# Reordering the first row of attention before a long matrix product: values between scores, a last block on ScalarE, and the dilated half of x first

## The chip, the cores and the metric

The kernel runs on one core of a Trainium2 chip. The metric is the device time of one execution in microseconds (us). Executions of one kernel agree within about half a microsecond to two microseconds here, so every comparison below is between runs taken in the same rounds on the same chip. The parts of the core that matter are TensorE (PE in the profile; PEld is its weight load), VectorE (DVE), ScalarE (ACT), GpSimd (POOL), SyncE (SP), and the DMA engines.

## The reference

Attention over eight batch elements ("rows" 0 to 7 below), eight heads of 64 columns, 576 tokens, followed by a feed-forward layer with a squared ReLU.

```python
mask_plain = (rel >= 0) & (rel < 32)                        # heads 0-3: "sliding"
mask_dil   = (rel >= 0) & (rel < 128) & (rel % 4 == 0)      # heads 4-7: "dilated"
attn = softmax(where(mask, q @ k.T / 8, -1e9))              # per row and head
x = (attn @ v).transpose(0, 2, 1, 3).reshape(4608, 512)     # 8 rows x 576 tokens
h = x @ w_in                                                # 512 -> 2048
return (relu(h) ** 2) @ w_out                               # 2048 -> 512
```

## The kernel before

The feed-forward layer takes tokens in chunks of 512. Its first product, mm1, makes `ph` from `xT`, which is x transposed, in four blocks of 128 columns. Blocks 0 and 1 are the sliding half (transposed into PSUM, an on-chip memory, as `px`, then copied by ScalarE), and blocks 2 and 3 are the dilated half (`py`, copied the same way). `po`, and `poa` to `poe`, are results of the second product; VectorE combines them (`u`), and `otl` and `otu` are parts of the output that are then stored. While one chunk's products run, the attention of the next row is woven in: `pump(n)` advances the products by n steps, a step being two matmuls of mm1 or four of the second product. In rows 2 to 7, `attn_values` calls a small function between its pieces (a fill), and that function pumps.

```python
def mm1_gen(c, g, sm=None):                 # chunk c
    xs = xT[:, :, c * TOKC : (c + 1) * TOKC]
    for ffc in range(NFF):                  # 16 blocks of w_in
        ph = pmool.tile(...)
        for dmk in range(NDM):              # 0, 1 sliding; 2, 3 dilated
            nc.tensor.matmul(ph, wi[:, dmk, ...], xs[:, dmk, :],
                             start=(dmk == 0), stop=(dmk == NDM - 1))
            if dmk == 1:
                yield
        relu_squared(c, ffc, g, ph, rts)
        # ... cut
        yield

def normalize(b, what, pav, w, n=2):        # divide by the softmax's sum, on VectorE
    # ... cut: x, rcp, pv
    nc.vector.reciprocal(rcp[0:w, 0:n], pv[:, :, :, D])
    nc.vector.tensor_tensor(out=x[0:w, 0:n], in0=pv[:, :, :, 0:D], in1=rcp..., op=ALU.mult)
```

Row 0 has nothing to run beside. It is a prologue, with idle matmuls (`pj`) that have no use but to keep TensorE busy. Its second half reads as follows; `s_` are scores, `av_` value products with their normalization, and `x_` the transposes and copies.

```python
    s_sliding_half(0, 1)
    s_sliding_half(1, 1)
    cast_dilated_v(nc.gpsimd, DIL, (1,)); cast_sliding_v(nc.gpsimd, 3, 3, 6)
    constants_late()
    idle(8)
    zs = av_dilated(0, 1, 0)
    x_dilated(0, 0, ys, False)
    zs += av_dilated(0, 1, 1)
    xs += av_sliding(0, 3, 5)
    xs += av_sliding(0, 5, 6)
    idle(16); x_dilated(0, 1, zs, False)
    idle(16); x_sliding(0, 1, xs, False)
    idle(12)
    # ... then mm1 of chunk 0, with row 1's attention woven in
```

The softmax here doesn't subtract the row's maximum and nothing guards it: scores larger than these inputs give would overflow.

## Time and profile before

| | before |
|---|---|
| median of the first three runs | 307.59 us (306.98 to 307.77) |
| profiled execution: first to last instruction | 306.2 us, mean granted clock 0.997 |
| TensorE busy | 97% |
| first `ph` of row 0's chunk | 25.29 us |
| from it to the first `ph` after row 1 | 37.43 us |
| from the end of VectorE's last instruction to the end | 4.3 us |

The table reads in the order of the program. TensorE has no free time worth speaking of, so the time of the kernel is a sum: the prologue to 25.29 us, then matmuls, then what TensorE waits for between them, then an ending after the last matmul.

### The profile page before, as it was taken

Reading aid. Unit: us, or ns where it says so; the run is one execution under the profiler, and the core shown is the slowest. Engines: PE = TensorE matmul, PEld = TensorE weight load, DVE = VectorE, ACT = ScalarE, POOL = GpSimd, SP = SyncE. Lnnn points to the kernel's source line nnn. Section 1 sums busy time; section 2 is a strip of 40 time slices with the busy share of each in tenths; the row PEclk is TensorE's granted clock in tenths of the full one; section 3 lists DMA queues with packets and bytes.
Section 4 is the critical chain, followed back from the end, with each engine's and each line's share of the span. In section 5 each row is a group of like instructions: output and inputs, shape, how many; then the busy total and the mean of one; then the engine's idle time right before and its main releaser. Section 6 shows DMA issues by size and latency. Waiting matters only on the chain.

```text
span 306.2 us, 7007 instructions
## 1 busy us (share of the span) xinstructions
PE 295.5 (97%) x2898; PEld 192.3 (63%) x2898; DVE 208.6 (68%) x410; ACT 184.4 (60%) x304; POOL 49.7 (16%) x98
## 2 busy tenths in 40 slices
PE   7989999999998999999999999999999999999993
PEld 3766444444795469646964696469646974784583
DVE  4662375679975797679767976797669775743843
ACT  6565776678925992499248934893489346306610
POOL 7465000208005000410041003200100010000000
PEclk9999999999999999999999999999999999999998
DMA  8999997899989999889938983999410021003013
GB/s 172 223 213 228 235 206 155 154 174 220 317 180 273 222 177 222 256 161 206 225 128 173 228 204 119 181 195 199 144 44 0 2 88 51 2 0 137 2 34 104
DMA packets 85615, 47.89 MB, mean 156 GB/s; under 512 B 68112, under 2 KB 82896, under 8 KB 85200
## 3 DMA queue, kind: packets, MB, share of 16 engines
q1 hardware_dynamic: 76688, 27.24, 41.2%
q0 software_dynamic: 8352, 19.80, 29.2%
q10 hardware_dynamic: 544, 0.43, 0.5%
q8 instruction: 22, 0.36, 0.5%
q14 instruction: 9, 0.07, 0.1%
HBM read 39.85 MB, written 16.52 MB: 184 GB/s over the span
## 4 chain that ended last, share of the span: by engine, by line
PE 90%; DMA 2%; DVE 2%; ACT 2%; issue 1%; POOL 1%; ACTq 0%; POOLq 0%
PE ph L380 41%; PE poa L430 9%; PE pob L430 9%; PE pod L430 5%; PE poe L430 4%; PE poc L430 4%; PE po L401 3%; DMA early<-in_q_dram 2%; PE paw L764 2%; PE pav L747 2%; PE pz L667 2%; PE ps L648 1%; PE pj L530 1%; PE px L779 1%; PE py L797 1%
## 5 line engine op out<-in xcount | busy, mean ns | idle before, releaser
L380 PE MATMUL ph<-xT,wi 128*128 128x512 f16 x576 | 130.0, 379 | 0.3 <-ACT xT L803 0.3
L346 ACT ACTIVATE rt<-ph 128x512 f16<-128x512 f32 x144 | 84.9, 601 | 36.2 <-PE ph L380 35.9
L380 PEld LDWEIGHTS <-wi 128*128 128x128 f16 x576 | 54.4, 98 | 63.0 <-issue 0.8
L350 DVE TENSOR_TENSOR g<-rt 128x1024 f16<-128x1024 f16 x63 | 43.6, 692 | 46.4 <-ACT rt L346 46.2
L430 PEld LDWEIGHTS <-sm 128*128 128x128 f16 x512 | 46.9, 98 | 4.8
L430 PEld LDWEIGHTS <-g 128*128 128x128 f16 x384 | 36.0, 98 | 6.9 <-DVE g L348 1.3
L430 PE MATMUL pob<-T,sm 128*128 128x256 f16 x256 | 32.8, 272 | 0.0
L430 PE MATMUL poa<-wo,g 128*128 128x256 f16 x256 | 32.6, 273 | 0.0
L450 POOL DMA_DIRECT2D out_dram<-otl x6 | 4.6, 761 | 149.2 <-DVE otl L485 132.3
L803 ACT COPY xT<-py 128x576 f16<-128x576 f16 x16 | 10.2, 639 | 27.9 <-PE py L797 27.7
L728 DVE TENSOR_TENSOR x_d<-paw,rcp_d 72x512 f16<-72x512 f32 x32 | 22.0, 686 | 1.1
L785 ACT COPY xT<-px 128x576 f16<-128x576 f16 x16 | 10.3, 641 | 14.6 <-PE px L779 14.5
L620 ACT ACTIVATE AT<-pz 128x576 f16<-128x576 f32 x28 | 16.7, 649 | 1.9 <-PE pz L667 1.5
L401 PE MATMUL po<-wo,g 128*128 128x512 f16 x64 | 17.8, 379 | 0.0
L728 DVE TENSOR_TENSOR x_p<-pav,rcp_p 96x512 f16<-96x512 f32 (+1 forms) x25 | 16.6, 665 | 0.9
L620 ACT ACTIVATE AT<-ps 128x576 f16<-128x576 f32 x28 | 16.7, 649 | 0.8 <-PE ps L630 0.4
L430 PE MATMUL poe<-wo,sm 128*128 128x256 f16 x128 | 16.5, 273 | 0.0
L430 PE MATMUL poc<-T,sm 128*128 128x256 f16 x128 | 16.4, 272 | 0.0
L727 DVE RECIPROCAL rcp_d<-paw 72x8 f32<-72x8 f32 x32 | 6.3, 197 | 14.6 <-PE paw L764 14.6
L430 PE MATMUL pod<-T,g 128*128 128x256 f16 x128 | 16.1, 272 | 0.0
L621 DVE TENSOR_TENSOR AT<-AT,maskp 128x576 f16<-128x576 f16 x28 | 12.7, 457 | 2.8 <-ACT AT L620 1.8
L470 ACT COPY otu<-poa 128x512 f32<-128x512 f32 x8 | 4.7, 586 | 16.1 <-PE poa L430 16.1
(119 smaller groups left out, 352.0 us busy)
## 6 DMA issues: line engine op xcount, KB each, us to landing
sv<-in_v_dram SPq DMA_DIRECT2D x40, 128.0 KB, 4.7
sd<-in_v_dram SPq DMA_DIRECT2D x8, 512.0 KB, 6.8
dk<-in_k_dram POOLq DMA_DIRECT2D x12, 288.0 KB, 6.1
dk<-in_q_dram POOLq DMA_DIRECT2D x12, 288.0 KB, 7.5
out_dram<-otl POOLq DMA_DIRECT2D x6, 512.0 KB, 3.3
out_dram<-otu POOLq DMA_DIRECT2D x6, 512.0 KB, 4.3
sd<-in_v_dram SPq DMA_DIRECT2D x8, 288.0 KB
wi<-in_moe_w_in_dram POOLq DMA_DIRECT2D x4, 512.0 KB, 9.9
```

What stands on the lines that cost most here:

```text
L346: nc.scalar.activation(rt[:, o, :], ph[:], ACTF.Relu)
L350: nc.vector.tensor_mul(g[:, ffc - 1 : ffc + 1, :], rt, rt)
L380: nc.tensor.matmul(ph, wi[:, dmk, ffc * P : ffc * P + P], xs[:, dmk, :], start=(dmk == 0), stop=(dmk == NDM - 1),)
L401: nc.tensor.matmul(po, g[:, ffc, t * P : (t + 1) * P], wo[:, ffc, :], start=(ffc == 0), stop=(ffc == NFF - 1),)
L430: nc.tensor.matmul(acc, lhs[:, k, t * P : (t + 1) * P], rhs[:, k, :], start=(first and k == 0), stop=(k == NK - 1), skip_group_check=True,)
L620: nc.scalar.activation(AT[:, u, 0:UW], ps[:, :, 0 : UW // 2], ACTF.Exp, scale=scale)
L621: nc.vector.tensor_mul(AT[:, u, 0:UW], AT[:, u, 0:UW], mask)
L667: nc.tensor.matmul(ps[:, e, QD * n : QD * (n + 1)], QKTd[r, 1, a, q0 - PADD : q0 - PADD + P], QKTd[r, 0, a, q0 : q0 + QD], start=True, sto ...
L727: nc.vector.reciprocal(rcp[0:w, 0:n], pv[:, :, :, D])
L728: nc.vector.tensor_tensor(out=x[0:w, 0:n], in0=pv[:, :, :, 0:D], in1=rcp[0:w, 0:n].unsqueeze(3).to_broadcast([w, n, HH, D]), op=ALU.mult,)
L785: nc.scalar.copy(xT[:, 0:2, t0 : t0 + 288], px[:, 0:UW].rearrange("x (c t) -> x c t", c=2),)
L803: nc.scalar.copy(xT[:, 2:4, t0 : t0 + 288].rearrange("x c (i r) -> x c i r", r=DIL), py[:, 0:UW].rearrange("x (c r i) -> x c i r", c=2, r= ...
```

## The change

The intent is to shorten the prologue. The first value product of the second half goes between the two late score tiles. The last block of 96 tokens is normalized by four ScalarE instructions instead of one on VectorE. The last cast of q is split by head pairs over GpSimd and VectorE. And mm1 takes the dilated blocks first, because in row 0 the dilated half is ready before the sliding half. A slower pumping at the end of row 2 is added to go with the new order of mm1.

```diff
@@ the last cast, split
-    cast_sliding_qk_half(0, 1, nc.gpsimd)
+    cast_sliding_qk_pair(0, 1, 1, nc.gpsimd)
 ...
     ys = av_dilated(0, 0, 0)
+    cast_sliding_qk_pair(0, 1, 0, nc.vector)
@@ mm1
-            for dmk in range(NDM):
+            for n, dmk in enumerate((2, 3, 0, 1)):
 ...
-                    start=(dmk == 0), stop=(dmk == NDM - 1),
+                    start=(n == 0), stop=(n == NDM - 1),
@@ normalize
-    def normalize(b, what, pav, w, n=2):
+    def normalize(b, what, pav, w, n=2, eng=None):
 ...
+        if eng is nc.scalar:
+            for h in range(HH):
+                nc.scalar.mul(x[0:w, 0, h, :], pv[:, 0, h, 0:D], rcp[0:w, 0, h : h + 1])
+            return [x[:, 0]]
@@ row 0, second half
     s_sliding_half(0, 1)
-    s_sliding_half(1, 1)
     cast_dilated_v(nc.gpsimd, DIL, (1,))
     cast_sliding_v(nc.gpsimd, 3, 3, 6)
-    constants_late()
-    idle(8)
+    idle(4)
     zs = av_dilated(0, 1, 0)
+    s_sliding_half(1, 1)
     x_dilated(0, 0, ys, False)
+    idle(4)
     zs += av_dilated(0, 1, 1)
     xs += av_sliding(0, 3, 5)
-    xs += av_sliding(0, 5, 6)
+    xs += av_sliding(0, 5, 6, nc.scalar)
+    constants_late()
     idle(16)
@@ rows 2 to 7
-        attn_values(b, lambda: pump(2))
+        n_val[0] = 0
+        def rows():
+            n_val[0] += 1
+            pump(1 if b == 2 and n_val[0] > 7 else 2)
+        attn_values(b, rows)
```

(Cut: the definition of the split cast, and the passing of `eng` through `av_sliding`.)

More of the change, by code (lines that the diff above doesn't have):

```diff
@@ L184, in cast_sliding_qk_half, with cast_sliding_qk_pair @@
             sq[:, i, :, 192 * f : 192 * (f + 1)].rearrange("p h (j d) -> p j h d", d=D),
+        )
+    def cast_sliding_qk_pair(i, f, hp, eng):
+        hs = slice(2 * hp, 2 * hp + 2)
+        copy(
+            eng,
+            nqh[:, f, i, :, hs, :],
+            sq[:, i, hs, 192 * f : 192 * (f + 1)].rearrange("p h (j d) -> p j h d", d=D),
         )
@@ L383, in mm1_gen @@
                     xs[:, dmk, :],
-                    start=(dmk == 0),
-                    stop=(dmk == NDM - 1),
+                    start=(n == 0),
+                    stop=(n == NDM - 1),
                 )
-                if dmk == 1:
+                if n == 1:
                     yield
@@ L734, in normalize, with av_sliding @@
         return [x[:, i] for i in range(n)]
-    def av_sliding(b, m0, m1):
+    def av_sliding(b, m0, m1, eng=None):
         if m1 - m0 == 2:
@@ L753, in av_sliding @@
                 )
-        return normalize(b, f"p{m0}", pav, QB, m1 - m0)
+        return normalize(b, f"p{m0}", pav, QB, m1 - m0, eng)
     def av_dilated(b, t, a):
```

## The prediction

> **What bounds the kernel now.** I began with the page's first part, busy time by engine.
>
> ```profile
> PE 295.5 (97%) x2898; PEld 192.3 (63%) x2898; DVE 208.6 (68%) x410; ACT 184.4 (60%) x304; POOL 49.7 (16%) x98
> ```
>
> TensorE is the bound. A change can pay only where TensorE waits, or runs matmuls that exist to keep it busy. I then asked for the busy time of stretches cut where a token chunk's first product (ph) begins, and kept these four. The first two numbers are the stretch's length and TensorE's busy time.
>
> ```profile
> 0.00:25.29 25.29, 21.30 (x334) 15.24 (x335) 13.69 (x44) 15.14 (x27) 15.12 (x30) 1.00 1.11 202
> ...
> 62.72:95.25 32.53, 31.68 (x320) 21.13 (x318) 27.14 (x52) 21.37 (x35) 7.69 (x11) 1.00 1.01 230
> 95.25:125.85 30.60, 30.60 (x315) 20.69 (x315) 22.84 (x44) 20.23 (x33) 3.47 (x9) 1.00 1.06 223
> 125.85:156.73 30.88, 30.88 (x318) 20.81 (x316) 23.54 (x45) 20.23 (x33) 4.62 (x10) 1.00 0.85 191
> ```
>
> From 95 us on TensorE has no hole until the last store. The end is therefore the start of ph at 25.29, plus fixed work, plus the holes before 95 us. Row 0 (the first batch element's attention) is the prologue, a chain of latencies padded with idle matmuls. The chain that ended last shows its tail:
>
> ```profile
> 18.38 0.57 issue
> 19.80 0.55 PE pj L530 x8
> 20.88 0.69 DVE x_d L728
> 21.72 0.54 PE pav L747 x12
> 22.26 0.89 PE pj L530 x16
> 23.41 0.90 PE pj L530 x16
> 24.60 0.65 ACT xT L785
> 25.29 13.97 PE ph L380 x64
> ```
>
> Two waits and 44 idle matmuls set 25.29. The value product pav waits for its PSUM buffer, which VectorE's scaling x_d frees. After it come 16 idle matmuls, a transpose, 16 idle, the last transpose (px) and its copy xT, for which ph waits while 12 idle matmuls run.
>
> Last, the timeline at the ends of rows 1 and 2, for the reordered product:
>
> ```profile
> 61.72 1.40 ACT L803 COPY xT<-py 128x576 f16<-128x576 f16 x2
> ...
> 62.01 0.43 PE L797 MATMUL py<-ident,x_d 72*128 72x72 f16 x8
> ...
> 62.72 0.59 PE L380 MATMUL ph<-xT,wi 128*128 128x512 f16 x2
> ...
> 93.47 0.69 DVE L728 TENSOR_TENSOR x_d<-paw,rcp_d 72x512 f16<-72x512 f32 x1
> ...
> 94.22 0.30 PE L797 MATMUL py<-ident,x_d 72*128 72x72 f16 x4 [0.55 <-DVE x_d L728]
> 94.36 0.60 PE L380 MATMUL ph<-xT,wi 128*128 128x512 f16 x2
> 94.56 0.64 ACT L803 COPY xT<-py 128x576 f16<-128x576 f16 x1 [0.79 <-PE py L797]
> 95.25 4.91 PE L380 MATMUL ph<-xT,wi 128*128 128x512 f16 x22 [0.29 <-ACT xT L803]
> ```
>
> In every row after row 0 the dilated half of x (copied from py) lands last, and ph takes the sliding half first. Two ph matmuls, 0.43 us at 0.216 each, hide the copy: wholly at 62.72 (the copy ends at 63.12, the third ph is due at 63.15), and in part at 94.36. In row 0 alone the sliding half lands last.
>
> **What the Trainium skill says.** (1) "TensorE: Matmul & The Clock Gate", Back-to-back issue gap: warm spacing N/2.4 + 2.5 ns, so 216 ns at 512 columns and 56 at 128. The trace agrees: 64 ph matmuls in 13.81 us (216 ns), 16 idle ones in 0.89 us (56). (2) "ScalarE: Activation LUTs", What ACT_TABLE_LOAD costs: 186 ns + 0.833 N, some 93 ns more per pointer operand, and 93 ns of overlap between neighbours. The trace has a 576-column copy at 0.64 us (formula 0.67), a 288-column one at 0.40 (0.43), and two of these in 0.70, an overlap of 0.10. No run so far shows the pointer term. (3) "Runtime: NRT & Kernel Launch", Instruction fetch mechanics: instructions arrive by DMA in blocks of 256. The "issue" gap of 0.57 us, in the middle of six alike score matmuls, after some 441 TensorE instructions and with the DMA full, looks like a late block; the trace does not prove it.
>
> **The change, part by part.**
>
> *Casts.* GpSimd casts half of the last q block, some 0.45 us for 0.82, and issues the second pair of w_in loads some 0.37 us sooner. VectorE takes the other half, some 0.5 us, at 15.5 between two scalings. Its next product is due at 16.27, so both casts land in time. Gain on the path: 0.
>
> *Values between the scores.* The first late score tile (ps) still runs at 18.95 and its exponential at 19.25 to 19.87. Now the first value product (paw) follows after 4 idle matmuls, at 19.34 instead of 20.19. VectorE scales it from 20.0 to 20.7, and the second paw finds its buffer free at 20.97. But the second score tile, moved behind the first paw, needs the PSUM buffer that the exponential frees: it starts at 19.92, its scores at 20.27, its exponential at 20.62 to 21.26. So pav starts at 21.30, not 21.72. Gain: 0.42.
>
> *Last block on ScalarE.* VectorE ends the second x_d at 22.35, the next scaling at 23.18, the last reciprocal at 23.27. Before, one VectorE instruction of 0.42 us followed. Now four ScalarE instructions of 64 columns and a pointer scale do: an estimate from page (2), 186 + 53 + 93 = 0.33 us each, 0.24 apart, together 1.05 us, or 0.6 if the pointer is free. They end at 23.9 to 24.35; VectorE would have ended at 23.7. The transposes of px, which could start at 23.72 by the idle count, wait for them. Loss: 0.2 to 0.6.
>
> *Dilated half first, row 0.* ph need not wait for xT after the 12 idle matmuls: 25.29 - 25.05 gives 0.24. So: px done at 24.0 to 24.4, 12 idle matmuls (0.65), ph at 24.65 to 25.07. Row 0 gains 0.22 to 0.64; I take 0.4. The masks' copies, moved behind this, are off the path.
>
> *Dilated half first, later rows.* Row 1: ph waits for the copy, 63.12 plus 0.05 of semaphore, instead of starting at 62.72: loss 0.45. Row 2: now 95.25, where uninterrupted matmuls would have had to start at 95.25 - 0.43 = 94.82: loss 0.43. The slower pumping of row 2 leaves eight poe matmuls (0.87 us) to cover the copy. But VectorE is busy without a hole from 89.05 to 94.16, ending in the x_d that the last py waits for, and the order of its work does not change. TensorE only waits before py instead of after it: those eight run from 94.36 to 95.23 and ph starts at 95.25 all the same. Worth: 0. Row 3 already has eight poe matmuls there; its copy ends at 125.65, ph is due at 125.69: 0. Rows 4 to 7 end with tokens which the next chunk does not read: 0.
>
> *Sum*: 307.6 - 0.4 + 0.45 + 0.43 = 308.1.
>
> **The rivals.** (a) *The row 2 pumping works*, because paw and py find their operands sooner than I read. For it: the tweak is so specific that someone must have seen it pay. Against it: the continuous VectorE row. Then 307.6. (b) *The fetch gap goes or shrinks*, since the loads around it move by 0.37 us and blocks arrive by the same DMA. Row 0 then gains up to 0.6 more: 307.5, or 307.0 with (a). It could as well grow: 308.5. (c) *A transfer takes the gain*: row 1's inputs are issued on landings, not on TensorE's progress. The sd load lands near 54.2 and its second cast is due at 54.9; QKTx lands at 69.1 for scores at 71.03. The least slack is 0.7 us, more than I expect row 0 to gain, so this costs 0 to 0.1. (d) *ScalarE's four small scalings delay the py copy behind them in order.* That copy then ends near 24.9, before ph at 25.07, so it costs nothing unless they exceed 1.2 us.
>
> **Range and chances.** Parts of a tenth to half a microsecond cancel, with an uncertain sum of about ±0.6. My arithmetic says 308.1. I shade it to 307.8, as the kernel is tuned and (a) and (b) pull down more than up. The three runs before spread by 0.8 us. The range is 306.8 to 308.6. Two per cent is 6.2 us, a quarter of the prologue, and no part is near that: faster 0.01, same 0.98, slower 0.01.
>
> **What would show it.** Right: pav starts 0.3 to 0.5 us sooner; four ScalarE instructions last 0.6 to 1.1 us together and end after 23.8; the first ph is at 24.6 to 25.1 with no wait for xT inside it; TensorE has a new hole of about 0.45 us before ph at the end of row 1; the holes of row 2 grow from 0.85 to about 1.3 us, all before the last py. Wrong: the fetch gap moved by over 0.3 us, no hole at the end of row 1, or ph of row 2 less than 0.2 us later, counted from row 1's ph and uninterrupted matmuls. A time below 306.8 would mean that row 0 gained over 1.6 us if the later losses stand, or that they do not exist.

## The result

| | before, same rounds | changed |
|---|---|---|
| median | 307.41 us (306.98 to 307.77, 4 runs) | 307.15 us (307.06 to 307.27, 4 runs) |
| ratio, 95% interval | | 0.9992 (0.9975 to 1.001): the same within 2% |
| profiled execution | 306.2 us, clock 0.997 | 305.4 us, clock 0.999 |

Ratios here and below are the mean time of one kernel's fast runs over the mean of the other's fast runs of the same rounds, so they are not quite the ratios of the medians that are quoted. The result is inside the predicted range and in the class that was given 0.98. The sum on which it rested, however, was 308.1, and that sum is not what the profile shows.

The busy line of the page after answers the first view of the prediction.

```profile
PE 296.0 (97%) x2898; PEld 192.3 (63%) x2898; DVE 208.8 (68%) x410; ACT 185.0 (61%) x308; POOL 47.9 (16%) x98
```

ScalarE has the four new instructions (304 to 308), VectorE has one less scaling and one more cast (410 and 410), and GpSimd is 1.8 us less busy. TensorE's share is unchanged.

The next two views are the busy time by stretch, cut where a chunk's first `ph` begins: first the one stretch of before that the prediction left out, then the changed kernel. The columns are the stretch, its length, then busy time and number of instructions of PE, PEld, DVE, ACT and POOL, the granted clock, the DMA share and GB/s.

```profile
25.29:62.72 37.43, 36.38 (x317) 17.85 (x316) 20.57 (x43) 25.27 (x42) 6.57 (x15) 1.00 0.97 188
```

```profile
0.00:24.62 24.62, 21.55 (x334) 15.31 (x335) 13.72 (x44) 15.50 (x31) 14.58 (x29) 1.00 1.10 205
24.62:62.53 37.91, 36.57 (x320) 17.83 (x318) 21.00 (x43) 26.02 (x44) 6.77 (x16) 1.00 0.97 189
62.53:95.05 32.52, 31.26 (x317) 20.84 (x317) 26.12 (x50) 20.91 (x34) 5.81 (x11) 1.00 1.02 229
95.05:125.66 30.61, 30.61 (x316) 20.57 (x314) 23.33 (x45) 20.01 (x33) 3.88 (x9) 1.00 1.07 213
```

Row 0 is 0.67 us shorter (25.29 to 24.62). Row 1 is 0.48 longer (37.43 to 37.91). Row 2 seems as long as before (32.53 and 32.52), but the cut of before lies at the third `ph`, because two had run ahead of the wait; counted from 94.82, where uninterrupted matmuls would have begun, before took 32.10 and the changed kernel 0.42 more. From 95 us on the two run alike: the stretch from this `ph` to the one near 249 us is 154.36 us before and 154.38 after. All in all the changed kernel's last VectorE instruction ends 0.24 us *later* (301.89 before, 302.13 after). It is then the ending that is shorter, by a microsecond.

TensorE's timeline of row 0 after, cut to the steps that count. The columns are start, length, engine and line, operation, what it writes and reads, shapes, count, and in brackets the idle time before it with its releaser.

```profile
17.87 0.41 PE L689 MATMUL ps<-biasp,ident 128*128 128x288 f16 x2
18.21 0.57 PE L703 MATMUL ps<-QKTp 64*128 64x96 f16 x6
...
18.95 0.42 PE L776 MATMUL paw<-vd,AT 128*128 128x65 f16 x8
19.52 0.41 PE L689 MATMUL ps<-biasp,ident 128*128 128x288 f16 x2 [0.15 <-ACT AT L695]
...
20.91 0.56 PE L759 MATMUL pav<-vp,AT 128*128 128x65 f16 x12
...
23.90 0.22 PE L791 MATMUL px<-ident,x_p 96*128 96x96 f16 x1 [0.17 <-ACT x_p L738]
23.95 0.83 PE L538 MATMUL pj<-zz 128*128 128x128 f16 x12
24.62 0.38 PE L388 MATMUL ph<-xT,wi 128*128 128x512 f16 x1
```

Each planned move is there. `paw` follows the first score tile, the second tile waits a little for the exponential's buffer, `pav` starts at 20.91 without a wait (21.72 and a wait of 0.59 us before), and `ph` follows the twelve idle matmuls with no wait for `xT`. Against that stands the wait at 23.90, for ScalarE's scaling:

```profile
22.93 0.91 ACT L738 ACTIVATE x_p<-pav,rcp_p 96x64 f16<-96x64 f32 x4 [1.55 <-DVE rcp_p L735]
```

Four small ScalarE instructions took 0.91 us, where the one on VectorE took 0.42. The transposes `px` began at 23.35 and stalled between the fifth and the sixth until 23.90.

One thing more is in row 0. In the profiled execution of before, TensorE paused for about 0.75 us inside the six score matmuls of the first late tile; in this one it paused for about 0.27. That is 0.48 us of the 0.67.

The ends of rows 1 and 2, the same timeline:

```profile
61.63 0.60 PE L409 MATMUL po<-wo,g 128*128 128x512 f16 x2
62.53 1.02 PE L388 MATMUL ph<-xT,wi 128*128 128x512 f16 x4 [0.29 <-ACT xT L815]
...
94.01 0.30 PE L809 MATMUL py<-ident,x_d 72*128 72x72 f16 x4 [1.17 <-DVE x_d L740]
94.15 1.04 PE L438 MATMUL poe<-wo,sm 128*128 128x256 f16 x8
95.05 0.59 PE L388 MATMUL ph<-xT,wi 128*128 128x512 f16 x2
```

In row 1, two `po` matmuls from 61.63 on would have let `ph` start at 62.07; it starts at 62.53, because it now needs the dilated half, which is copied last. In row 2 the wait before the last `py` is 1.17 us instead of 0.55. Eight `poe` matmuls now cover the copy, but they used to run before that `py`; the idle time has moved and grown, not gone.

Last, the ending. This view lists what SyncE waited for, by the line of the end of the program: total us, times, longest. First before, then after.

```profile
SPq L1030 <- DMA out_dram<-otu: 1.7, 2, 1.4
...
SPq L1030 <- DMA out_dram<-otl: 1.2, 1, 1.2
```

```profile
SPq L1050 <- DMA out_dram<-otl: 1.0, 1, 1.0
...
SPq L1050 <- DMA out_dram<-otu: 0.6, 2, 0.3
```

The wait for the last stores of `otu` is 0.6 us in place of 1.7. Nothing in the change touches those stores.

### The profile page after: what moved, and what is told of

It reads as the page before. It is cut to its first block, busy times and chain, and to the rows that moved or that the text cites. A ratio compares the mean times of both kernels' runs of the same rounds, so it can differ in the third digit from the quotient of the medians.

```text
span 305.4 us, 7012 instructions
## 1 busy us (share of the span) xinstructions
PE 296.0 (97%) x2898; PEld 192.3 (63%) x2898; DVE 208.8 (68%) x410; ACT 185.0 (61%) x308; POOL 47.9 (16%) x98
## 4 chain that ended last, share of the span: by engine, by line
PE 89%; DMA 3%; DVE 2%; ACT 2%; POOL 2%; issue 1%; ACTq 0%; POOLq 0%
PE ph L388 42%; PE poa L438 9%; PE pob L438 9%; PE pod L438 5%; PE poe L438 4%; PE poc L438 4%; PE po L409 3%; DMA early<-in_q_dram 3%; PE paw L776 2%; PE pav L759 2%; PE pz L675 2%; PE ps L656 1%; PE px L791 1%; PE py L809 1%; POOL early L119 1%; DVE x_d L740 1%
```

## The experiments

Twelve kernels were run, all with correct results, each with five rounds, beside runs of before in the same rounds. "End" below is the time from the end of VectorE's last instruction to the end of the execution. The questions are taken one after the other.

### 1. Is the ending, or the pause in row 0, chance? Before, once more

No edit: the kernel before.

> The kernel before, unchanged, as a control. If the 0.48 us by which the pause inside the first late score tile shrank (0.75 us to 0.27 us) belongs to the change, this run has 0.75 again and its first ph at 25.3. If it is chance of the run (the rival), the pause comes out anywhere from 0.2 to 0.9 us and the first ph moves with it, between 24.7 and 25.4. The time from the last VectorE instruction to the end of the span was 4.3 us before and 3.3 us after; as nothing there was changed, I expect it to scatter between these. Ratio to before 1.000.

Measured: 307.93 us (307.46 to 308.39) beside 307.46, ratio 1.0007 (0.9995 to 1.0019). The end was 4.30 us, as in the first profile. The pause was gone, as this line of TensorE's timeline shows:

```profile
18.39 0.30 PE L695 MATMUL ps<-QKTp 64*128 64x96 f16 x6
```

Six score matmuls take 0.30 us here, without a hole. So the pause differs between executions of one kernel, and the difference that it made between the two first profiles can't be credited to the change. The end is not chance: I had thought that it might scatter between 3.3 and 4.3 us, and it did not. Over all fourteen profiles the pause lies between 0 and 0.75 us without any pattern by kernel. It always falls at one place, between TensorE's 220th and 221st matmul. What causes it was not found; that a late block of TensorE's instructions does would fit a fixed place, but remains a guess.

### 2. What does the order of mm1 cost and give?

**The order alone** on the kernel before, for every chunk:

```diff
-            for dmk in range(NDM):
+            for n, dmk in enumerate((2, 3, 0, 1)):
```

> The kernel before with nothing but the new order of the first product, in all chunks. My theory: ph of row 0 no longer waits for xT (0.24 us gained), ph of row 1 waits 0.45 us for the dilated copy and ph of row 2 starts 0.43 us later; ScalarE has its old number of instructions, so the stretch from the last VectorE instruction to the end stays 4.3 us. Sum 0.64 us slower than before. Rival (the order is what makes the changed kernel faster): 0.3 us faster than before.

Measured: 308.19 us (307.96 to 309.19) beside 307.47, ratio 1.0026 (1.001 to 1.0043). In row 0 `ph` started at 24.52 with no wait for `xT`, 3.36 us after `pav` (21.16) where the second run of before had 3.57: a gain of 0.21. In row 1 it waited for the copy and lost 0.46 us (the row was 0.62 us longer; the other 0.16 was a wait for a copy of q and k, see rival (c) below), in row 2 the idle time before `ph` was 0.73. The end was 4.28. This is the predicted balance of 0.24 gained and about 0.9 lost, and the ending of before.

**The order for chunk 0 only**, in the changed kernel:

```diff
-            for n, dmk in enumerate((2, 3, 0, 1)):
+            for n, dmk in enumerate((2, 3, 0, 1) if c == 0 else range(NDM)):
```

> The changed kernel, but only chunk 0 takes the dilated half first; the slower pumping of row 2 stays. My theory: the hole of 0.46 us at the end of row 1 goes, the first ph stays where the change put it, and row 2 stays as it is, because its copy ends only when the eight poe matmuls do. So 0.45 us faster than the changed kernel, 306.7. Rival (the order costs nothing): same as the changed kernel, 307.15.

Measured: 306.63 us (306.39 to 308.09) beside 307.46, ratio 0.9977 (0.996 to 0.9994). The hole before `ph` at the end of row 1 is gone (`po` at 62.84, `ph` at 63.28, which is two matmuls later). The profiled execution was the slowest of the six, since row 1 lost some 0.9 us in it to a late cast and a late copy of q and k, so its span (306.3) is not used.

**Even pumping of row 2**, in the changed kernel:

```diff
-            pump(1 if b == 2 and n_val[0] > 7 else 2)
+            pump(2)
```

> The changed kernel with row 2 pumped evenly, so that the pumping is the only part undone. My theory: the pumping is worth nothing while the dilated half goes first: ph of row 2 starts within 0.05 us of where it does in the changed kernel, counted from ph of row 1, and the time is the same, 307.15. Rival: slower by 0.4 to 0.9 us, as the eight poe matmuls no longer cover the copy.

Measured: 307.12 us (306.95 to 307.87) beside 307.46, ratio 0.9989 (0.9977 to 1.0001). TensorE's timeline shows the wait where it would be without the tweak:

```profile
94.88 0.81 PE L388 MATMUL ph<-xT,wi 128*128 128x512 f16 x3 [0.73 <-ACT xT L815]
```

From row 1's `ph` (62.37) this is 32.51 us; with the slower pumping it was 32.52. The slower pumping moves the wait from `ph` to `py` and is worth nothing, as predicted. This run had no pause in row 0, and neither had the second run of before, so the two give row 0 cleanly: from the start of the first late score tile to `ph` it is 6.49 us (17.98 to 24.47) against 6.72 (18.05 to 24.77). The changes to row 0 together are worth 0.23 us. The part up to `pav` took 2.77 us (to 20.75) against 3.15 (to 21.20): values between the scores are worth 0.38. The part from `pav` to `ph` took 3.72 against 3.57, so it is longer, though `ph` no longer waits for the copy.

**Both edits:**

> As order_row0, and row 2 is pumped evenly as in the kernel before. My theory: row 2 returns to a hole of 0.85 us instead of 1.27, since two ph matmuls run while the copy is made; in all 0.88 us faster than the changed kernel, 306.3. Rival (the slower pumping of row 2 is what hides the copy): slower than order_row0 by some 0.4 us.

Measured: 306.66 us (305.97 to 306.72), ratio 0.9965 (0.9952 to 0.9978), 0.0024 below even pumping alone, which is some 0.7 us. The expected 306.3 was missed, and the median is no better than with the order for chunk 0 alone (306.63). In the profiles, however, row 2 went as expected: it took 32.10 us again (61.82 to 93.92, counted as above), against 32.52 with the order for chunk 0 alone (63.28 to 95.80). So the order of mm1 in chunks 1 and 2 costs the changed kernel 0.7 to 0.9 us, and everything else in it made it faster than before by more than I had allowed for.

### 3. What shortens the ending?

The trace records the packets of each DMA queue. In the last microseconds there is one that no store accounts for. In this view, a slice of 0.2 us of before (303.6 to 303.8) and one of 0.5 us of the changed kernel (301.5 to 302.0), the columns are the queue and its kind, packets, MB and the share of 16 engines.

```profile
q14 instruction: 1, 0.01, 9.7%
```

```profile
q14 instruction: 1, 0.01, 6.1%
```

It is a packet of 8192 bytes of instructions. I then took from the traces where it starts, when the last packet of a store ends, and how many records (waits included) VectorE and ScalarE have in all; times are us before the end of the execution.

| kernel | VectorE records | ScalarE records | instruction packet starts | last store packet ends | end |
|---|---|---|---|---|---|
| before | 450 | 412 | 2.46 | 2.15 | 4.30 |
| before, again | 450 | 412 | 2.46 | 2.14 | 4.30 |
| the order alone | 450 | 412 | 2.46 | 2.14 | 4.28 |
| changed | 451 | 416 | 3.59 | 1.49 | 3.30 |
| even pumping | 451 | 416 | 3.50 | 1.49 | 3.21 |
| order of chunk 0 | 451 | 416 | 3.73 | 1.56 | 3.44 |
| both | 451 | 416 | 3.52 | 1.51 | 3.22 |

SyncE's last wait for the stores ends some 1.1 us before the end in every trace that I compared. In the kernels with the long end, the packet starts as the data of the last store (ScalarE's) end, the last store packet (4 bytes, of the same store) comes directly behind it, and SyncE's wait ends 1.08 us after that one. In the kernels with the short end the packet comes over a microsecond sooner, while SyncE is still issuing, and the wait ends 0.41 to 0.50 us after the last store packet. Up to the last packet of data nothing differs: from ScalarE's issue of its store to that packet's end it is 1.80 us in before and 1.78 in the changed kernel. The whole microsecond lies behind it, 1.39 us against 0.42. The theory is that some engine's instruction stream crosses a boundary near the end, and that the change shifts it. GpSimd's records are 158 and SyncE's 168 in both kernels, VectorE's and ScalarE's differ. Four kernels ask whose stream it is.

**ScalarE's?** Four one-column copies on ScalarE, early in the kernel before:

```diff
+    spare = const.tile([P, 4], FP32, name="spare")
+    for i in range(4):
+        nc.scalar.copy(spare[:, i : i + 1], zz[:, i : i + 1])
```

> The kernel before plus four one-column ScalarE copies into a spare tile near the start, where ScalarE waits for input. They do no work that counts. My theory, formed from the traces: the changed kernel's end is 1.0 us shorter because its ScalarE stream is four instructions longer, so that the last 8 KB instruction packet is fetched before the last store instead of during it. Then this kernel too has 3.3 us from the last VectorE instruction to the end, not 4.3, and is 1.0 us faster than before. Rival (the end is shorter for another reason, or by chance): 4.3 us, same time as before.

Measured: VectorE 450, ScalarE 416; the packet starts 2.45 us before the end, the end is 4.0 us. ScalarE's count is the changed kernel's, and the packet has not moved: it is not ScalarE's stream. The time was 306.63 us (305.46 to 307.55) beside 307.47, ratio 0.9971 (0.995 to 0.9991). Only 0.3 us of that gain is in the ending, where the data of ScalarE's store took 1.53 us from its issue and not 1.80. In the profiled execution row 0's late scores began at 17.39 instead of about 18.0, and across the runs that start lies anywhere from 17.39 to 18.67; whether the copies helped it or these six runs were lucky is open.

**SyncE's?** Eight more small loads issued by SyncE:

```diff
+    extra = const.tile([1, 8, D], FP32, name="extra")
+    for i in range(8):
+        nc.sync.dma_start(out=extra[:, i, :], in_=q[0, 0, i : i + 1, :])
```

> The kernel before plus eight loads of 256 bytes each into a spare tile, issued by SyncE in row 0 while its queue is idle. My theory: the packet at the end is the last block of SyncE's own instructions, and SyncE stands waiting for it when the data of the last stores have long landed. Eight more SyncE instructions bring that fetch forward, so the stretch from the last VectorE instruction to the end is 3.3 us or less, and the time 1.0 us less than before. Rival (the packet is another engine's, or only goes along with the wait): packet still 2.46 us before the end, 4.0 to 4.3 us, same time as before.

Measured: 307.77 us (307.21 to 308.1) beside 307.44, ratio 1.0003 (0.9988 to 1.0018). SyncE has 176 records instead of 168; the packet starts 2.47 us before the end, the end is about 4.3. Not SyncE's stream.

**The split cast?** It adds one instruction to VectorE. Its function and its two calls alone, on before:

```diff
-    cast_sliding_qk_half(0, 1, nc.gpsimd)
+    cast_sliding_qk_pair(0, 1, 1, nc.gpsimd)
...
     ys = av_dilated(0, 0, 0)
+    cast_sliding_qk_pair(0, 1, 0, nc.vector)
```

> The kernel before with nothing but the last cast by head pairs on two engines. On the path of row 0 I valued it at 0, and still do. The four ScalarE copies did not move the last 8 KB instruction packet, so the ScalarE count is not what shortens the end; in every kernel with the split cast, and in none without it, that packet starts some 3.5 us before the end instead of 2.46 and the stretch from the last VectorE instruction to the end is 3.2 to 3.4 us instead of 4.0 to 4.3. If the split cast is the part that does it, this kernel has 3.3 us there and is 1.0 us faster than before. Rival (one of the other parts does it): 4.3 us, same time as before.

Measured: 307.25 us (306.96 to 307.65) beside 307.44, ratio 0.9991 (0.9979 to 1.0003); end 4.28, packet 2.46 us before the end. The cast was added, but a wait went away with it, and VectorE's records stayed at 450. The time agrees with the prediction's zero for the casts. As to the ending, it leaves VectorE's stream possible but does not show it.

**VectorE's?** Three one-column memsets on VectorE, early in the kernel before:

```diff
+    spare = const.tile([P, 3], FP32, name="spare")
+    for i in range(3):
+        nc.vector.memset(spare[:, i : i + 1], 0.0)
```

> The kernel before plus three one-column VectorE memsets of a spare tile near the start, where VectorE is idle. Neither four ScalarE instructions nor eight SyncE loads nor the split cast moved the last 8 KB instruction packet. What is left that goes with it in all runs is the number of VectorE instructions in the trace: 450 where the packet comes 2.46 us before the end, 451 to 453 where it comes some 3.5 us before it. My theory: the packet is a block of VectorE's stream, so this kernel has it at 3.5 us, 3.3 us from the last VectorE instruction to the end, and is 1.0 us faster than before. Rival (the number only happens to go along with it): packet at 2.46 us, 4.0 to 4.3 us, same time as before; then what moves the packet stays open.

Measured: 306.37 us (305.7 to 306.69) beside 307.38, ratio 0.9966 (0.9952 to 0.998). VectorE has 453 records and the other engines the numbers of before; the packet starts 3.60 us before the end, the end is 3.25. Rows 0 to 2 are as in before (from the first `ph`, 24.60, to the two that run ahead in row 2, 93.70, it is 69.10 us, and 69.07 in before). The view of SyncE's waits:

```profile
SPq L1033 <- DMA out_dram<-otl: 1.0, 1, 1.0
...
SPq L1033 <- DMA out_dram<-otu: 0.6, 2, 0.3
```

These are the numbers of the changed kernel. Three instructions with no use, which no other instruction needs, make the kernel before about a microsecond faster (0.0034 of 307.4 is 1.05 us). The ratio alone would not show why, for the four copies on ScalarE measured nearly the same one (0.9971) without moving the packet. The traces do: three more instructions on VectorE moved the packet, and more on ScalarE or SyncE did not, so it is a block of VectorE's instructions. The end is 4.00 to 4.31 us in the six profiles with the late packet and 3.19 to 3.44 in the eight with the early one, about 1.0 us apart. That the packet itself holds up the stores fits its place directly before the last store packet, but no run moved the one without the other.

### 4. Is there a version that beats both?

**The last block back on VectorE**, with both edits of part 2:

```diff
-    xs += av_sliding(0, 5, 6, nc.scalar)
+    xs += av_sliding(0, 5, 6)
```

> order_row0_even_pump with the last block of row 0 scaled on VectorE again, so four ScalarE instructions fewer. My theory: px no longer waits for ScalarE and the first ph starts some 0.33 us sooner, counted from the first late score tile and without the pause in it; but the end is 4.3 us again instead of 3.2. Net 0.7 us slower than order_row0_even_pump. Rival without the end effect: 0.33 us faster than it.

Measured: 306.12 us (305.56 to 307.2) beside 307.47, ratio 0.9958 (0.9937 to 0.9978). TensorE's timeline:

```profile
23.45 0.42 PE L791 MATMUL px<-ident,x_p 96*128 96x96 f16 x6
23.70 0.83 PE L538 MATMUL pj<-zz 128*128 128x128 f16 x12
24.38 0.59 PE L388 MATMUL ph<-xT,wi 128*128 128x512 f16 x2
```

The six transposes run without a stall. With its pause of 0.22 us taken off, row 0's late part is 6.14 us (18.02 to 24.38), against 6.49 with ScalarE's scaling, a cost of 0.35; and from `pav` (21.00) to `ph` it is 3.38, against 3.72, a cost of 0.34. The end stayed short at 3.19, with ScalarE's records back at 412 and VectorE's at 452. The theory of ScalarE's stream, under which this kernel should have lost 0.7 us against the pair of edits, missed.

**Pumping less earlier in row 2**, with the order for chunk 0 only:

```diff
-            pump(1 if b == 2 and n_val[0] > 7 else 2)
+            pump(1 if b == 2 and 4 <= n_val[0] <= 6 else 2)
```

> order_row0, but row 2 pumps once instead of twice at its fourth, fifth and sixth fills and not at its eighth to tenth. VectorE then finishes the second pob product after the second paw has been scaled, as in rows 3 to 6. My theory: the last x_d of row 2 comes 1.2 us sooner, py does not wait, the eight poe matmuls cover the copy, and row 2 has no hole of more than 0.1 us before ph. 0.85 us faster than order_row0_even_pump, 1.3 us faster than order_row0. Rival (VectorE's total work, not its order, sets row 2): same as order_row0_even_pump.

Measured: 305.70 us (304.94 to 307.04) beside 307.47, ratio 0.9943 (0.9922 to 0.9963). VectorE at the end of row 2, then TensorE:

```profile
91.81 0.69 DVE L740 TENSOR_TENSOR x_d<-paw,rcp_d 72x512 f16<-72x512 f32 x1
92.42 0.68 DVE L492 TENSOR_TENSOR u<-poc,u 128x512 f32<-128x512 f32 x1
```

```profile
92.87 1.04 PE L438 MATMUL poe<-wo,sm 128*128 128x256 f16 x8
93.75 1.03 PE L388 MATMUL ph<-xT,wi 128*128 128x512 f16 x4
```

The last `x_d` is now ahead of the combinations `u` and `otl` of the second product's `poc` in VectorE's order. In the changed kernel it came behind both, at 93.27:

```profile
93.27 0.69 DVE L740 TENSOR_TENSOR x_d<-paw,rcp_d 72x512 f16<-72x512 f32 x1
```

The value products come sooner because fewer steps of the second product lie before them. TensorE has no hole at all in row 2, which takes 30.92 us (62.83 to 93.75), 1.18 less than with both edits of part 2 (32.10). This is what the tweak of the change could have been: the slower pumping has to come before VectorE's queue has filled, not at its end.

**All of it**: the order for chunk 0 only, the earlier slow pumping, the last block on VectorE, and eight instead of twelve idle matmuls before the first `ph`:

```diff
-    idle(12)
+    idle(8)
```

> The changed kernel with four corrections: only chunk 0 takes the dilated half first; row 2 pumps once at its fourth to sixth fills; the last block of row 0 is scaled on VectorE; the last idle matmuls are 8, not 12. Against pump_earlier my theory gives 0.33 us for px without its wait and 0.22 us for the four idle matmuls, with ph of chunk 0 running on without a wait for xT: 305.1 us. Rival (the row 0 gains are hidden by the copies of xT): ph waits inside, same as pump_earlier, 305.7 us.

Measured: 305.06 us (303.94 to 305.91) beside 307.44, ratio 0.9916 (0.9897 to 0.9934). The first `ph` starts at 23.92 without a wait, row 2 has no hole, and the end is 3.43 us. This version beats both kernels, by 2.4 us over before. By the limit of 2% that too is "the same".

## Why the prediction was right or wrong

The range and the class were right, the range in part by luck: the sum was 308.1, the measured time 307.15, and what lay between was not foreseen. One term was missing in the sum, and it is larger than all the others. With the chance of the pause taken out, by the runs of part 2 and 4, the account is this:

| term | predicted | measured | where |
|---|---|---|---|
| values between the scores | -0.42 | -0.38 | start of scores to `pav`, second run of before and even pumping |
| last block on ScalarE | +0.2 to +0.6 | +0.34 | `pav` to `ph`, even pumping and last block on VectorE |
| dilated half first, row 0 | -0.24 | -0.21 | `pav` to `ph`, the order alone |
| row 0 together | -0.4 (-0.22 to -0.64) | -0.23 | |
| casts | 0 | 0 | the casts alone: -0.19 in the median, interval over zero |
| dilated half first, row 1 | +0.45 | +0.46 | changed kernel and the order alone |
| dilated half first, row 2 | +0.43 | +0.42 | changed kernel |
| slower pumping in row 2 | 0 | 0 | 32.52 with it, 32.51 without |
| rows 3 and on | 0 | 0 | 154.36 and 154.38 us |
| the ending | not in the sum | -1.0 | both profiles (4.30 and 3.30), three memsets on VectorE |

The measured terms add up to -0.35. The change measured -0.26 in the medians (-0.25 by the ratio), and with even pumping, which leaves all the terms as they are, -0.34. That is agreement within the intervals, which are about half a microsecond either way.

**The step that failed** is this sentence of the prediction: "The end is therefore the start of ph at 25.29, plus fixed work, plus the holes before 95 us." The work from 95 us to the last matmul is fixed, and the trace bears that out to a few hundredths. What follows the last matmul is not fixed. In the kernel before, a block of VectorE's instructions arrived inside the last store, between its data and its last packet; in the changed kernel it arrived before that store's data. The changed kernel has 451 records on VectorE instead of 450; the one more is a wait (38 instead of 37). That the block belongs to VectorE is shown by the three memsets, and that an early block goes with an end shorter by 1.0 us by all fourteen profiles. Why the completion of the stores takes 1.08 us behind the block and 0.41 to 0.50 otherwise is not shown, nor which part of the change added the wait: the split cast alone did not.

**The row 0 terms** were each nearly right; their sum was at the low end of the range given. I took the middle of it. That range did not follow from the terms: 0.42 and 0.24 less a loss of 0.2 to 0.6 is 0.06 to 0.46, while 0.22 to 0.64 came from the times at which `px` would end, and these allow a loss of 0.02 to 0.44 only. The marks that I had set were met: `pav` 0.38 us sooner once the pause is out, four ScalarE instructions in 0.91 us that ended at 23.84, the first `ph` at 24.62 without a wait for `xT`. The last one owes 0.48 us to the smaller pause; without that, `ph` would have come at 25.1, the late end of the mark. The casts cost 0.50 us on GpSimd and 0.65 on VectorE, where 0.45 and 0.5 were assumed, and both were in time.

**Rows 1 and 2** went as written, to a few hundredths: a new hole of 0.46 us before `ph`, and in row 2 idle time of 1.26 us (32.52 less 31.26) in place of 0.85, of which 1.17 is before the last `py`.

**The shading from 308.1 to 307.8** had two reasons, and neither held. Rival (a), that the slower pumping works, is refuted by even pumping. Rival (b), a smaller pause, did occur in the profiled run, and my mark "wrong: the fetch gap moved by over 0.3 us" was hit, by 0.48. But the second run of before had no pause at all, so it differs between executions of one kernel, and nothing shows that the change moved it. That the shading brought the number closer to the result was luck: its reasons were not the cause. Rivals (c) and (d) did not show in the changed kernel: the rows after row 0 started no later for a transfer, and ScalarE's `py` copy was off the path. But something like (c) does occur: in the profiles of four other kernels TensorE waited longer than usual in row 1 for the cast or copy of q and k, and the row grew by 0.16 (the order alone), 0.23 (pumping less earlier), 0.26 (all of it) and 0.87 us (the order for chunk 0). Why there is open.

**The first citation** leaves something out. In the Trainium skill, "TensorE: Matmul & The Clock Gate", the section Back-to-back issue gap gives N/2.4 + 2.5 ns for an isolated matmul; for a real stream of weight loads and matmuls it gives about 131 ns at 512 columns. The 64 `ph` matmuls of the trace are such a stream and took 216 ns each: the formula fits here, and the stream figure does not.

**In hindsight**, the sign of the whole change turns on something that nothing in the diff aims at. Without the ending, the terms of the table make it slower by some 0.65 us (an estimate: -0.23 + 0.46 + 0.42), since the new order of mm1 is right for one chunk, where the dilated half lands first, and wrong for the two next, where it lands last.

## What to carry to other kernels

Let a product take first the operand that lands first, and decide it for each instance: an order that is right in a prologue cost 0.9 us in the two chunks after it. When a wait is to be covered, find which instruction of the releasing engine ends it and what is queued ahead of that one; slower pumping four calls sooner changed VectorE's order and removed 1.2 us, at the end it removed nothing. A difference of a microsecond between two nearly equal kernels went here with where an instruction block arrived, so compare the endings of both traces and try a few useless instructions on the engine in question before giving a change the credit.

## What the Trainium skill lacked or had wrong

- "Runtime: NRT & Kernel Launch", Instruction fetch mechanics, calls the cost of crossing a block boundary "mostly hidden". Here one crossing appears exposed: 1.0 us went with whether a block of VectorE's instructions came 2.46 or 3.6 us before the end (three added memsets: end 3.25 us in place of 4.30). The page has nothing on the last stores as a place where a crossing shows.
- The same section gives blocks of 16 KiB. The traces have packets of 16384 bytes in one instruction queue (22 of them; TensorE's, to judge by the number, as no other engine has a tenth of its instructions) but of 8192 bytes in the queue that carried VectorE's block.
- "ScalarE: Activation LUTs", What ACT_TABLE_LOAD costs: nearly right. By the page's rule, an instruction of 64 columns with a pointer scale takes 332 ns (an estimate) and neighbours overlap by 93 ns. Here one took 306 ns, and four took 0.91 us, an overlap of 0.10 us. No run had the same instruction without the pointer, so its term alone is not shown.
- No page has the case of an instruction packet that comes directly before the last packet of a store: SyncE's wait then ended 1.08 us after that last packet, and 0.41 to 0.50 us after it otherwise.
